# Delta-rule attention with a mixture of experts: the column steps of one block's triangular inverse move from VectorE to GpSimd

## The chip, the core and the metric

The kernel runs on one core of a Trainium2 chip. A core has five engines, each with its own instruction queue that is worked off in order: TensorE (PE in the profile; PEld is its weight load), VectorE (DVE), ScalarE (ACT), GpSimd (POOL) and SyncE (SP), which only issues DMAs here. They meet through semaphores. All work on SBUF, an on-chip memory of 128 partitions; PE writes its results to PSUM, which DVE and ACT read. The metric is device time in microseconds (us). The kernel before took 501.41 us, the median of three runs (498.14 to 501.8).

## What is computed

For 32 pairs of batch and head, a state of 48x48 is carried through 768 positions (q, k, v of 48 features each, beta one number):

```python
k_n = k / (np.linalg.norm(k, axis=-1, keepdims=True) + 1e-06)
for t in range(S):
    y[:, :, t] = np.einsum('bhd,bhde->bhe', q[:, :, t], state)
    v_old = np.einsum('bhde,bhd->bhe', state, kt)
    state = state + bt[:, :, :, None] * np.einsum('bhd,bhe->bhde', kt, vt - v_old)
```

The 3072 rows of the result (384 wide) then go through a mixture of 8 experts: the largest of 8 logits picks an expert, `relu(x @ w1) @ w2` (1024 hidden) is computed by that expert, and the row is scaled by its softmax weight.

## The kernel before

The 768 positions are cut into 6 time blocks of 128, and each block into 4 pieces of 32. Inside a piece the recurrence is a triangular system; its inverse is computed beforehand for all 32 pairs and the 4 pieces of a block at once (tile `wt`, 128 partitions by 32x32). The main loop has 27 ticks (`for t in range(NN + LAG)`); tick t starts the four pieces of one batch of block t // 4, so that block tb is needed from tick 4 tb on. A tick has seven slots, `beside(t, 0)` to `beside(t, 6)`, and `place` counts them (7t + i). Per tick:

- PE multiplies state and keys (`residual`, L442 and L454), DVE subtracts the product from the values (L461, one instruction a tick), PE multiplies with the inverse (`apply`, L469, needs `wt`), ACT copies the result to tile `u` (L473, into a tile that POOL has cleared, L431), and PE makes outputs and states from it (L492, L503, L512) and the next masks (L279; POOL masks them, L290). PE's products of the router (`xp`, L536) and of the block after next (L279, `pg`) stand between one tick's L454 and its L469.
- Beside it a block's inverse is worked out on DVE, cut into small steps that are put between the others. `prepare` makes norms and diagonals (L303 `ss`, a square root on ACT at L307, then L325 to L340, L349) from tile `lg`, which a DMA brings (L269); `lanes` has a first scaling (L377) and then 14 pairs of column steps (L382: product into `tmp`; L385: sum into `lw`, each needing the one before), then the corner: a copy (L390), six products (L401) and six sums (L407), and the transpose into `wt` (L412).
- The router's small steps run on POOL up to tick 16 (L648 to L696), and it scatters the rows with indirect DMAs (L544).

Order: everything is issued by the Python program in this order; no scheduler moves it. `ROOT[tb]` gives three places for a block: where its `ss` is taken, where the square root is issued, and where the rest of `prepare` may begin. In each slot `inverses` issues steps up to a budget (0.9 of the program's own units); two blocks at a time may be open and then take turns. A block's transpose isn't issued before tick 4 tb - 1, and what is left of a block at tick 4 tb is issued there at once. After the loop come the eight experts, where PE is nearly always busy.

Of the kernel before, what the change touches and what calls it, by code (L numbers as in the profile page):

```python
# [13 lines left out]
ALU = mybir.AluOpType  # L14
# [27 lines left out]
def deltanet_moe(ctx, tc, kt_d, qt_d, kn_d, v_d, beta_d, w_gate, w1, w2, out):  # L42
    nc = tc.nc
# [75 lines left out]
    LAG = NB - 1  # L119
    FILL = 'k4 k5 k6 k7', 'k1 q0 k2 k3', 'k8 k9', 'k10 k11 q1'  # L120

    ROOT = {1: (-1, -1, -1), 2: (17, 20, 22), 3: (38, 41, 43), 4: (66, 69, 71), 5: (94, 97, 99)}
    INIT = (0, 1, 2, 3, 'l', 0)

    STEPS = (3, 3, 3, 2, 2, 2, 2)
# [56 lines left out]
    tiles = {tb: {b: {} for b in range(B)} for tb in range(NT)}  # L182
# [52 lines left out]
    def kpart(n):  # L235

        tb, b = n // B, n % B
        kt, gg = kt_t[n] if n < KTL else kg_t[n % KTG], gg_t[n % KSL]
        V, A = nc.vector.tensor_copy, nc.scalar.copy
        if tb == 0:  # L240
# [6 lines left out]
            for h in range(H):  # L247
                p, a = h // 2, h % 2
                r = slice(64 * a, 64 * a + 64)
                for i in range(NB):  # L250
                    t = slice(32 * i, 32 * i + 32)
                    nc.tensor.matmul(db[a][t, p, :], lhsT=kt[r, p, t], rhs=kt[r, p, t], start=True, stop=True,
                                     tile_position=(64 * a, 32 * i), skip_group_check=True)
            V(out=dg[:, b * H:(b + 1) * H:2], in_=db[0])
            A(out=dg[:, b * H + 1:(b + 1) * H:2], in_=db[1])
# [53 lines left out]
    def prepare(tb):  # L309
# [13 lines left out]
        ss, s0, r0 = (T[k] for k in ("ss", "s0", "r0"))  # L323
        V = nc.vector
        V.reciprocal(r0, s0)  # L325
        yield
        V.scalar_tensor_tensor(out=r0, in0=ss, scalar=0.25, in1=r0, op0=ALU.mult, op1=ALU.mult)
        yield
        V.scalar_tensor_tensor(out=s0, in0=r0, scalar=1e-6, in1=s0, op0=ALU.add, op1=ALU.add)
        yield  # L330
# [28 lines left out]
    def both_halves(t):  # L359

        def view(r, c, m, w):
            return bass.AP(tensor=t.tensor, offset=t.offset + 32 * r + c, ap=[list(t.ap[0]), [16 * 33, 2], [32, m], [1, w]])
        return view

    def lanes(tb):


        T = tiles[tb]
        lg, lw = T["lg"], T["lw"]
        G, W = both_halves(lg), both_halves(lw)  # L370
        V = nc.vector
        tmp = fp.tile([128, 128], F32, name=f"tmp{tb}", tag=f"tmp{tb % 2}")
        for c in range(15):
            m, w = 15 - c, c + 1
            if c == 0:
                for g in (0, 16):
                    V.tensor_scalar(out=lw[:, g + 1:g + 16, g], in0=lg[:, g + 1:g + 16, g], scalar1=lw[:, g, g:g + 1],  # L377
                                    scalar2=None, op0=ALU.mult)
                yield 0.4
                continue  # L380
            x = tmp[:, 0:2 * m * w].rearrange("p (g a b) -> p g a b", g=2, a=m)
            V.tensor_tensor(out=x, in0=G(w, c, m, 1).broadcast_to([128, 2, m, w]),  # L382
                            in1=W(c, 0, 1, w).broadcast_to([128, 2, m, w]), op=ALU.mult)
            yield 0.2 + m * w / 480
            V.tensor_tensor(out=W(w, 0, m, w), in0=W(w, 0, m, w), in1=x, op=ALU.add)  # L385
            yield 0.2 + m * w / 480
        big = [fp.tile([128, 1024], F32, name=f"big{i}_{tb}", tag=f"big{i}") for i in range(2)]

        first_, prod = lg[:, 0:16, 0:16], lg[:, 0:16, 16:32]
        V.tensor_copy(first_, lw[:, 0:16, 0:16].rearrange("p k a -> p a k"))  # L390
        yield 0.5
        work = []
        for a, b in ((0, 4), (4, 9), (9, 16)):
            work.append((first_[:, a:b, a:16], lg[:, 16:32, a:16], prod[:, a:b], False))
        for a, b in ((12, 16), (7, 12), (0, 7)):
            work.append((lw[:, 16 + a:16 + b, 16:16 + b], prod[:, :, 0:b], lw[:, 16 + a:16 + b, 0:16], True))
        todo = []
        for i, (x, y, out, minus) in enumerate(work):
            m, n, k = x.shape[1], y.shape[1], x.shape[2]
            t = big[i % 2][:, 0:m * n * k].rearrange("p (m n k) -> p m n k", m=m, n=n)  # L400
            V.tensor_tensor(out=t, in0=x.unsqueeze(2).broadcast_to([128, m, n, k]),  # L401
                            in1=y.unsqueeze(1).broadcast_to([128, m, n, k]), op=ALU.mult)
            yield 0.15 + m * n * k / 960
            todo.append((out, t, minus))
            while len(todo) > (i not in (2, 5)):
                out, t, minus = todo.pop(0)
                V.tensor_reduce(out=out, in_=t, axis=AX.X, op=ALU.add, negate=minus)  # L407
                yield 0.15 + t.shape[1] * t.shape[2] * t.shape[3] / 960
        T["cols"] = True
        yield 0.0  # L410
        T["wt"] = lp.tile([128, BH, 32], F32, name=f"wt{tb}", tag="wt", bufs=2)
        V.transpose(out=T["wt"].rearrange("p h t -> p t h"), in_=lw)  # L412
        if tb + 2 < NT:
            clear_w(tb + 2)
        yield 2.0

    def scale_v(t, act=False):

# [521 lines left out]
    class Inverse:  # L940
# [6 lines left out]
        def steps(self):  # L947
            for _ in prepare(self.tb):
                yield 0.2
            yield 1.2  # L950
            self.at = 0
            yield from lanes(self.tb)

        def ready(self, t):
            if self.at == -12:
                return place[0] >= ROOT[self.tb][2]
            return not ("cols" in tiles[self.tb] and t < B * self.tb - 1)

        def step(self):
# [4 lines left out]
            self.at += 1  # L964
            return us

    line = [Inverse(tb) for tb in range(1, NT)]
    turn, owed, place = [None], [0.0], [-1]

# [5 lines left out]
    W = None  # L975

    def inverse_step(t):
        if not line:
            return None
        a = line[0]  # L980
        b = line[1] if len(line) > 1 and line[1].ready(t) else None
        ready = a.ready(t)
        if not ready and b is None:
            return None
        pair = ready and b is not None and "cols" not in tiles[a.tb]
        x = (b if turn[0] is a else a) if pair else a if ready else b
        turn[0] = x
        return x.step()

    def inverses(us, t):  # L990
        owed[0] += us
        while owed[0] > 0:
            got = inverse_step(t)
            if got is None:
                owed[0] = 0.0
                return
            owed[0] -= got
# [8 lines left out]
    def beside(t, i):  # L1006

        place[0] = 7 * t + i
        for tb in ROOT:
            if place[0] == ROOT[tb][0]:  # L1010
                squares(tb)
            if place[0] == ROOT[tb][1]:
                root(tb)
        inverses((SPEND0 if t < B else SPEND if t < 3 * B else SPEND2)[i], t)
        for _ in range(STEPS[i] if t < NN - B else 4):
            if fine and not run(fine[0]):
                fine.pop(0)
        for _ in range(WSL.count((t, i))):
            run(W)
        for _ in range(ES.count((t, i))):  # L1020
            ahead_step()

    fin = iter(())
    for t in range(NN + LAG):
        if t < NN and t % B == 0 and t > 0:
            while line and line[0].tb <= t // B:
                inverse_step(t)
            if t == NN - B:
# [3 lines left out]
                W = pieces()  # L1032
# [122 lines left out]
    V = nc.vector  # L1155
# [82 lines left out]
    op = ctx.enter_context(tc.tile_pool(name="op", bufs=1))  # L1238
# [10 lines left out]
    if True:  # L1249
# [3 lines left out]
        V = nc.vector  # L1253
# [107 lines left out]
```

## Time and profile before

| | |
|---|---|
| runs | 501.8, 498.14, 501.41 us |
| profiled execution | 498.63 us, its span 496.9 us |
| PE | 454.6 us (91%) |
| DVE | 321.2 us (65%) |
| ACT | 262.2 us (53%) |
| POOL | 166.1 us (33%) |
[...]

Shares are over the whole span. The loop takes about the first half of it; in tick 3 (61.6 to 70.1 us) DVE was busy for all of its 8.5 us and PE for 7.85, and from 41 to 209 us DVE was busy for 145 and POOL for 109 of 168 us.

### The profile page before, as it was taken

How to read it: one execution, taken by the hardware profiler on the slowest of the kernel's cores; microseconds unless marked ns; L12 is line 12 of the kernel's file. 1: busy time of each engine (PE TensorE's matmuls, PEld its weight loads, DVE VectorE, ACT ScalarE, POOL GpSimd, SP SyncE). 2: the span in 40 equal slices, each digit the busy share in tenths (PEclk: the TensorE clock that was granted, in tenths of full speed). 3: DMA queues.
4: the chain of work that ended last, by engine and by line, in shares of the span. 5: the costliest groups of instructions: out<-in, count | busy, mean ns of one | idle time of the engine just before them, and what ended most of it. 6: DMA issues, size and time to landing. Idle time of an engine off the chain costs nothing. (4 is left out here: it accounts for less than half of the span.)

```text
span 496.9 us, 17303 instructions
## 1 busy us (share of the span) xinstructions
PE 454.6 (91%) x7212; PEld 417.8 (84%) x7212; DVE 321.2 (65%) x726; ACT 262.2 (53%) x566; POOL 166.1 (33%) x338
## 2 busy tenths in 40 slices
PE   6768799989989799978899999999999999999995
PEld 4657678868778688866798999999999999999995
DVE  2899998797889989445544668274463647255330
ACT  2644876666757466666433456463553545354230
POOL 7003134767878878730211210201102020201111
PEclk9985999999999999979999899999999999999999
DMA  5999599783684353733302548464545646353101
GB/s 172 248 295 225 99 267 254 174 204 108 140 211 130 114 153 112 252 119 111 118 35 66 158 144 252 141 217 119 174 135 159 190 138 218 123 172 110 36 2 45
DMA packets 59228, 76.29 MB, mean 154 GB/s; under 512 B 26569, under 2 KB 45471, under 8 KB 59136
## 3 DMA queue, kind: packets, MB, share of 16 engines
q1 hardware_dynamic: 55680, 65.39, 47.5%
q0 software_dynamic: 3456, 9.57, 5.2%
q8 instruction: 71, 1.16, 1.0%
q14 instruction: 21, 0.17, 0.1%
HBM read 57.10 MB, written 18.62 MB: 152 GB/s over the span
## 5 line engine op out<-in xcount | busy, mean ns | idle before, releaser
L809 POOL DMA_INDIRECT out_dram<-yo,idx x32 | 30.7, 960 | 199.0 <-ACT yo L1140 118.2
L806 PE MATMUL y<-w2h,hx 128*128 128x384 f32 x352 | 93.5, 340 | 0.1
L729 DVE TENSOR_TENSOR w2l<-w2r,w2h 128x768 fp32r<-128x768 f32 x32 | 31.2, 978 | 74.7 <-ACT w2h L728 74.5
L806 PEld LDWEIGHTS y<-w2h,hx 128*128 128x128 f32 x352 | 64.1, 188 | 0.4 <-issue 0.4
L806 PE MATMUL y<-w2l,hx 128*128 128x384 f32 x176 | 59.3, 337 | 0.0
L795 PE MATMUL h<-xl,w1h 128*128 128x416 f32 (+2 forms) x168 | 57.3, 341 | 0.2 <-DVE xl L729 0.2
L795 PE MATMUL h<-xh,w1h 128*128 128x416 f32 (+2 forms) x168 | 57.3, 341 | 0.0
L795 PE MATMUL h<-xh,w1l 128*128 128x416 f32 (+2 forms) x168 | 57.2, 341 | 0.0
L473 ACT COPY u<-ks 32x384 f32<-32x384 f32 x96 | 45.1, 470 | 20.9 <-PE ks L469 18.8
L290 POOL TENSOR_SCALAR_AFFINE_SELECT pm<-pm 128x1024 f32<-128x1024 f32 x24 | 27.6, 1149 | 76.7 <-ACT pm L289 76.3
L798 ACT ACTIVATE hx<-h 128x448 fp32r<-128x448 f32 (+1 forms) x64 | 32.8, 517 | 32.6 <-PE h L795 29.3
L1140 ACT ACTIVATE yo<-y,gt 128x384 f32<-128x384 f32 x22 | 12.8, 582 | 69.9 <-PE y L806 57.0
L442 PE MATMUL ks<-st,kt 128*32 128x96 f32 x768 | 44.9, 253 | 2.4 <-ACT u L473 2.3
L799 DVE SCALAR_TENSOR_TENSOR hx<-h,hx 128x448 fp32r<-128x448 f32 (+1 forms) x64 | 36.8, 586 | 14.6 <-ACT hx L798 14.5
L442 PEld LDWEIGHTS ks<-st,kt 128*32 128x32 f32 x768 | 33.4, 111 | 6.3 <-ACT u L473 2.8
L544 POOL DMA_INDIRECT xg<-row,sli x24 | 29.4, 1224 | 25.5 <-ACT yt L516 8.0
L259 ACT COPY gg<-pg 128x512 f32<-128x512 f32 x48 | 25.8, 589 | 22.2 <-PE pg L279 22.2
L729 DVE TENSOR_TENSOR w1l<-w1r,w1h 128x1024 fp32r<-128x1024 f32 x24 | 29.4, 1224 | 9.9 <-ACT w1h L728 6.7
L469 PE MATMUL ks<-v_all,wt 32*32 32x48 f32 x1536 | 27.2, 207 | 9.2 <-DVE v_all L461 7.0
L469 PEld LDWEIGHTS ks<-v_all,wt 32*32 32x32 f32 x1536 | 22.3, 107 | 14.3 <-DVE v_all L461 9.0
L806 PEld LDWEIGHTS y<-w2l,hx 128*128 128x128 f32 x176 | 33.1, 188 | 0.0
L795 PEld LDWEIGHTS h<-xl,w1h 128*128 128x128 f32 x168 | 31.5, 188 | 0.6 <-DVE xl L729 0.5
(199 smaller groups left out, 1034.3 us busy)
## 6 DMA issues: line engine op xcount, KB each, us to landing
w1r<-in_w_dram SPq DMA_DIRECT2D x24, 512.0 KB
w2r<-in_w_dram SPq DMA_DIRECT2D x32, 384.0 KB
xg<-zrow SPq DMA_DIRECT2D x7, 788.0 KB
xr<-xg SPq DMA_DIRECT2D x7, 591.0 KB
ku<-in_kn_dram SPq DMA_DIRECT2D x20, 192.0 KB
qt<-in_qt_dram SPq DMA_DIRECT2D x36, 96.0 KB
kt<-in_kt_dram SPq DMA_DIRECT2D x34, 96.0 KB
v_all<-in_v_dram SPq DMA_DIRECT2D x15, 192.0 KB
```

The source lines that it names most:

```text
L259: A(out=gg[:, a:H:2], in_=pg[a])
L290: nc.gpsimd.affine_select(out=pm, in_=pm, compare_op=ALU.is_gt, fill=0.0, base=0, pattern=[[0, H], [1, C]], channel_multiplier=-1)
L442: nc.tensor.matmul(ks[32 * q:32 * q + 32, 2 * p:2 * p + 2, :], lhsT=kt_t[n % KTL][:, p, 32 * q:32 * q + 32], rhs=st_view(n % B, p), start= ...
L469: nc.tensor.matmul(ks[r, h, :], lhsT=tiles[n // B]["wt"][r, n % B * H + h, :], rhs=vn[r, h, :], start=True, stop=True, tile_position=(32 * ...
L473: nc.scalar.copy(out=uview(n)[r], in_=ks[r])
L544: put = nc.gpsimd.indirect_dma_start(out=xg, out_offset=bass.IndirectOffsetOnAxis(ap=at, axis=0), in_=x, in_offset=None, bounds_check=OFF ...
L729: nc.vector.tensor_tensor(out=lo, in0=src, in1=hi.bitcast(F32), op=ALU.subtract)
L795: nc.tensor.matmul(ps, lhsT=w[:, d, fs], rhs=x_[:, d], start=(n == 0), stop=(n == len(terms) - 1))
L798: nc.scalar.activation(out=hh, in_=ps, func=AF.Relu)
L799: nc.vector.scalar_tensor_tensor(out=hl, in0=ps, scalar=0.0, in1=hh.bitcast(F32), op0=ALU.max, op1=ALU.subtract)
L806: nc.tensor.matmul(ps, lhsT=h(f)[h_], rhs=w2[w][:, f, :], start=(n == 0), stop=(n == len(terms) - 1))
L809: nc.gpsimd.indirect_dma_start(out=out, out_offset=bass.IndirectOffsetOnAxis(ap=idx, axis=0), in_=yo, in_offset=None, bounds_check=N - 1, ...
```

## The change

Block 2 gets an entry in a table `COLS`. Its column steps are issued for POOL by `columns_beside`, from place 16 (tick 2, slot 2) on, five instructions per two slots; its corner stays on DVE and is issued only when all its column steps have been. All `ROOT` places move forward by 8 to 10 slots, and while block 2's `prepare` isn't done, it goes ahead of block 1's steps.

```diff
--- before.py
+++ after.py
@@ -119,7 +119,8 @@
     LAG = NB - 1
     FILL = 'k4 k5 k6 k7', 'k1 q0 k2 k3', 'k8 k9', 'k10 k11 q1'
 
-    ROOT = {1: (-1, -1, -1), 2: (17, 20, 22), 3: (38, 41, 43), 4: (66, 69, 71), 5: (94, 97, 99)}
+    ROOT = {1: (-1, -1, -1), 2: (8, 11, 13), 3: (28, 31, 33), 4: (58, 61, 63), 5: (86, 89, 91)}
+    COLS = {2: (16, 5, 2)}
     INIT = (0, 1, 2, 3, 'l', 0)
 
     STEPS = (3, 3, 3, 2, 2, 2, 2)
@@ -362,13 +363,13 @@
             return bass.AP(tensor=t.tensor, offset=t.offset + 32 * r + c, ap=[list(t.ap[0]), [16 * 33, 2], [32, m], [1, w]])
         return view
 
-    def lanes(tb):
+    def columns(tb):
 
 
         T = tiles[tb]
         lg, lw = T["lg"], T["lw"]
         G, W = both_halves(lg), both_halves(lw)
-        V = nc.vector
+        V, P = nc.vector, nc.gpsimd if tb in COLS else nc.vector
         tmp = fp.tile([128, 128], F32, name=f"tmp{tb}", tag=f"tmp{tb % 2}")
         for c in range(15):
             m, w = 15 - c, c + 1
@@ -379,11 +380,17 @@
                 yield 0.4
                 continue
             x = tmp[:, 0:2 * m * w].rearrange("p (g a b) -> p g a b", g=2, a=m)
-            V.tensor_tensor(out=x, in0=G(w, c, m, 1).broadcast_to([128, 2, m, w]),
+            P.tensor_tensor(out=x, in0=G(w, c, m, 1).broadcast_to([128, 2, m, w]),
                             in1=W(c, 0, 1, w).broadcast_to([128, 2, m, w]), op=ALU.mult)
             yield 0.2 + m * w / 480
-            V.tensor_tensor(out=W(w, 0, m, w), in0=W(w, 0, m, w), in1=x, op=ALU.add)
+            P.tensor_tensor(out=W(w, 0, m, w), in0=W(w, 0, m, w), in1=x, op=ALU.add)
             yield 0.2 + m * w / 480
+
+    def corner(tb):
+
+        T = tiles[tb]
+        lg, lw = T["lg"], T["lw"]
+        V = nc.vector
         big = [fp.tile([128, 1024], F32, name=f"big{i}_{tb}", tag=f"big{i}") for i in range(2)]
 
         first_, prod = lg[:, 0:16, 0:16], lg[:, 0:16, 16:32]
@@ -413,6 +420,10 @@
         if tb + 2 < NT:
             clear_w(tb + 2)
         yield 2.0
+
+    def lanes(tb):
+        yield from columns(tb)
+        yield from corner(tb)
 
     def scale_v(t, act=False):
 
@@ -949,11 +960,18 @@
                 yield 0.2
             yield 1.2
             self.at = 0
-            yield from lanes(self.tb)
+            if self.tb in COLS:
+                held[self.tb] = columns(self.tb)
+                yield next(held[self.tb])
+                yield from corner(self.tb)
+            else:
+                yield from lanes(self.tb)
 
         def ready(self, t):
             if self.at == -12:
                 return place[0] >= ROOT[self.tb][2]
+            if self.tb in held:
+                return False
             return not ("cols" in tiles[self.tb] and t < B * self.tb - 1)
 
         def step(self):
@@ -964,6 +982,15 @@
             self.at += 1
             return us
 
+    def columns_beside():
+
+        for tb in list(held):
+            n = ((place[0] - COLS[tb][0] + 1) * COLS[tb][1]) // COLS[tb][2] - ((place[0] - COLS[tb][0]) * COLS[tb][1]) // COLS[tb][2]
+            for _ in range(n if place[0] >= COLS[tb][0] else 0):
+                if tb in held and next(held[tb], None) is None:
+                    del held[tb]
+
+    held = {}
     line = [Inverse(tb) for tb in range(1, NT)]
     turn, owed, place = [None], [0.0], [-1]
 
@@ -983,7 +1010,7 @@
         if not ready and b is None:
             return None
         pair = ready and b is not None and "cols" not in tiles[a.tb]
-        x = (b if turn[0] is a else a) if pair else a if ready else b
+        x = (b if turn[0] is a or (b.tb in COLS and b.at < 0) else a) if pair else a if ready else b
         turn[0] = x
         return x.step()
 
@@ -1012,6 +1039,7 @@
             if place[0] == ROOT[tb][1]:
                 root(tb)
         inverses((SPEND0 if t < B else SPEND if t < 3 * B else SPEND2)[i], t)
+        columns_beside()
         for _ in range(STEPS[i] if t < NN - B else 4):
             if fine and not run(fine[0]):
                 fine.pop(0)
```

How it moves instructions, at three places. `v_all` with `ks` is the one subtraction of a tick; `lg`, `lw`, `ss`, `s`, `r`, `tmp` with the numbers 603, 634, 755 to 757, 892 to 894 and 907 belong to block 2, `lg_437`, `lw_155` and `big_1` to block 1, `lg_855` to block 3. Line numbers behind L119 are higher by 1 to 28 after the change.

DVE from tick 2's subtraction, before (down to tick 3's) and now (as many rows as reach block 1's corner):

```order
L461 TENSOR_TENSOR v_all<-v_all,ks_800 96x384
L401 TENSOR_TENSOR big_1_797<-lg_437 128x960
L407 TENSOR_REDUCE lg_437<-big_1_796 128x4x16
L401 TENSOR_TENSOR big_1_796<-lg_437 128x784
L303 TENSOR_SCALAR ss_892<-lg_603 128x32
L407 TENSOR_REDUCE lg_437<-big_1_797 128x5x16
L407 TENSOR_REDUCE lg_437<-big_1_796 128x7x16
L401 TENSOR_TENSOR big_1_797<-lw_155,lg_437 128x1024
L461 TENSOR_TENSOR v_all<-v_all,ks_914 128x384
```

```order
L472 TENSOR_TENSOR v_all<-v_all,ks_805 96x384
L326 RECIPROCAL r_757<-s_756 128x32
L328 SCALAR_TENSOR_TENSOR r_757<-ss_755,r_757 128x32
L330 SCALAR_TENSOR_TENSOR s_756<-r_757,s_756 128x32
L332 RECIPROCAL r_757<-s_756 128x32
L334 TENSOR_TENSOR ss_755<-bl,r_757 128x32
L337 TENSOR_TENSOR lw_634<-ss_755,r_757 128x32
L341 SCALAR_TENSOR_TENSOR lg_603<-lg_603,lw_634 128x16x16 x2
L350 STREAM_TRANSPOSE r_757<-s_756 128x32
L378 TENSOR_SCALAR lw_634<-lg_603,lw_634 128x15 x2
L408 TENSOR_TENSOR big_1_802<-lg_437 128x960
L414 TENSOR_REDUCE lg_437<-big_1_801 128x4x16
```

Block 2's whole `prepare` and its first scaling now stand between tick 2's subtraction and block 1's second product.

POOL in ticks 2 to 4, before and now (from the norms of block 2 on; 19 more column steps follow, with `u_997`, `pm_119` and then the clearing of `lw_1121` between or behind them):

```order
L431 MEMSET u_753 128x384
L431 MEMSET u_851 128x384
L290 AFFINE_SELECT pm_118<-pm_118 128x1024
L431 MEMSET u_971 128x384
L290 AFFINE_SELECT pm_119<-pm_119 128x1024
L296 MEMSET lw_1082 128x1024
```

```order
L355 COPY nt_all<-r_757 32x32 x4
L383 TENSOR_TENSOR tmp_907<-lg_603,lw_634 128x56
L386 TENSOR_TENSOR lw_634<-lw_634,tmp_907 128x2x14x2
L383 TENSOR_TENSOR tmp_907<-lg_603,lw_634 128x78
L386 TENSOR_TENSOR lw_634<-lw_634,tmp_907 128x2x13x3
L383 TENSOR_TENSOR tmp_907<-lg_603,lw_634 128x96
L386 TENSOR_TENSOR lw_634<-lw_634,tmp_907 128x2x12x4
L383 TENSOR_TENSOR tmp_907<-lg_603,lw_634 128x110
L386 TENSOR_TENSOR lw_634<-lw_634,tmp_907 128x2x11x5
L291 AFFINE_SELECT pm_118<-pm_118 128x1024
L383 TENSOR_TENSOR tmp_907<-lg_603,lw_634 128x120
```

The 28 column steps now stand in POOL's queue, around the clearing of tick 4's `u` and two masks.

DVE from tick 4's subtraction, with what each row waits for, before and now:

```order
L461 TENSOR_TENSOR v_all<-v_all,ks_1084 128x384 [waits DMAHW5_49,PE_49,Activation_49]
L336 TENSOR_TENSOR lw_634<-ss_892,r_894 128x32 [waits DVE_49]
L340 SCALAR_TENSOR_TENSOR lg_603<-lg_603,lw_634 128x16x16 [waits DVE_49]
L340 SCALAR_TENSOR_TENSOR lg_603<-lg_603,lw_634 128x16x16
L349 STREAM_TRANSPOSE r_894<-s_893 128x32
L538 TENSOR_REDUCE rl_0_1135<-xp_0_1136 128x8 [waits Activation_49]
L425 TENSOR_TENSOR v_all<-v_all,nt_all 128x384 [waits DMAHW2_49]
L377 TENSOR_SCALAR lw_634<-lg_603,lw_634 128x15 [waits DVE_49] x2
```

```order
L472 TENSOR_TENSOR v_all<-v_all,ks_1123 128x384 [waits DMAHW5_49,PE_49,Activation_49]
L304 TENSOR_SCALAR ss_1165<-lg_855 128x32 [waits DMAHW0_49]
L549 TENSOR_REDUCE rl_0_1170<-xp_0_1171 128x8 [waits Activation_49]
L436 TENSOR_TENSOR v_all<-v_all,nt_all 128x384 [waits DMAHW2_49]
L397 COPY lg_603<-lw_634 128x16x16 [waits Pool_49]
L408 TENSOR_TENSOR big_2_1195<-lg_603 128x1024 [waits DVE_49]
L408 TENSOR_TENSOR big_2_1196<-lg_603 128x960
L414 TENSOR_REDUCE lg_603<-big_2_1195 128x4x16 [waits DVE_49]
```

The copy that begins block 2's corner (L397 there) now waits for POOL, and stands in DVE's queue ahead of tick 5's subtraction, as do the corner's first three products and its first sum.

## Rows read from the trace of the kernel before

**Rows 1.** Timeline of DVE, ticks 0 to 5: start us, us, engine, line, operation, tiles.
```profile
41.18 0.52 DVE L461 TENSOR_TENSOR v_all<-v_all,ks 32x384 f32<-32x384 f32 x1
...
44.55 0.22 DVE L382 TENSOR_TENSOR tmp<-lg,lw 128x56 f32<-128x56 f32 x1
...
47.97 0.54 DVE L461 TENSOR_TENSOR v_all<-v_all,ks 64x384 f32<-64x384 f32 x1
...
54.63 0.54 DVE L461 TENSOR_TENSOR v_all<-v_all,ks 96x384 f32<-96x384 f32 x1
...
61.59 0.55 DVE L461 TENSOR_TENSOR v_all<-v_all,ks 128x384 f32<-128x384 f32 x1
...
70.13 0.53 DVE L461 TENSOR_TENSOR v_all<-v_all,ks 128x384 f32<-128x384 f32 x1
...
77.08 0.55 DVE L461 TENSOR_TENSOR v_all<-v_all,ks 128x384 f32<-128x384 f32 x1 [0.27 <-PE ks L454]
```

**Rows 2.** Timeline of DVE, corner of block 0, which no other work cuts into.
```profile
26.15 0.39 DVE L390 COPY lg<-lw 128x256 f32<-128x256 f32 x1
...
30.92 2.02 DVE L407 TENSOR_REDUCE lg<-big 128x80 f32<-128x960 f32 x2
```

**Rows 3.** Timeline of PE, the triangular products of ticks 4, 5 and 16.
```profile
70.72 0.45 PE L469 MATMUL ks<-v_all,wt 32*32 32x48 f32 x23 [0.43 <-DVE v_all L461]
...
79.08 0.70 PE L469 MATMUL ks<-v_all,wt 32*32 32x48 f32 x45
...
172.50 0.88 PE L469 MATMUL ks<-v_all,wt 32*32 32x48 f32 x64 [1.53 <-DVE v_all L461]
```

**Rows 4.** Waits of PE from 38 to 205 us: total us, times, longest us.
```profile
PE ks L469 <- DVE v_all L461: 3.2, 4, 1.5
...
PE pp L674 <- POOL oh_all L670: 1.6, 2, 0.9
```

**Rows 5.** POOL's two-input operations, two lines: duration ns min/median/max.
```profile
L648 POOL TENSOR_TENSOR m<-s x8: 195/196/337, 81.5 to 198.0; 128x2 f32<-128x2 f32 x8
...
L690 POOL TENSOR_TENSOR pos<-pos,oh_all x8: 218/219/1008, 88.8 to 203.6; 128x16 f32<-128x16 f32 x8
```

**Rows 6.** Timeline of POOL and DVE, two places where both are busy.
```profile
117.91 2.29 DVE L401 TENSOR_TENSOR big<-lg 128x1024 f32<-128x1024 f32 x2
...
118.02 1.16 POOL L648 TENSOR_TENSOR s<-oh 128x8 f32<-128x8 f32 x1
...
120.33 0.20 POOL L648 TENSOR_TENSOR m<-s 128x2 f32<-128x2 f32 x1
...
120.62 0.23 POOL L667 TENSOR_SCALAR m<-m 128x2 f32<-128x2 f32 x1
...
163.31 1.11 POOL L290 TENSOR_SCALAR_AFFINE_SELECT pm<-pm 128x1024 f32<-128x1024 f32 x1
...
163.34 1.49 DVE L425 TENSOR_TENSOR v_all<-v_all,nt_all 128x384 f32<-128x384 f32 x1
```

**Rows 7.** Timeline of PE, the same part of ticks 21 and 22.
```profile
209.59 0.88 PE L469 MATMUL ks<-v_all,wt 32*32 32x48 f32 x64
...
213.05 1.16 PE L279 MATMUL pq<-qt,kt 64*128 64x128 f32 x16
...
219.40 1.50 PE L469 MATMUL ks<-v_all,wt 32*32 32x48 f32 x64 [2.47 <-DVE v_all L461]
...
225.12 1.28 PE L279 MATMUL pq<-qt,kt 64*128 64x128 f32 x16
```

**Rows 8.** Stretch of 2 us: PE, PEld, DVE, ACT, POOL busy, granted clock, DMA.
```profile
220.00:222.00 2.00, 2.00 (x64) 1.74 (x52) 0.00 (x0) 0.13 (x1) 1.16 (x2) 0.50 0.77 194
```

**Rows 9.** Timeline of the DMA queue on SyncE.
```profile
27.52 0.34 SPq L269 DMA_DIRECT2D lg<-gd  x1
...
32.53 0.80 SPq L210 DMA_DIRECT2D ku<-in_kn_dram  x2
...
43.99 0.34 SPq L269 DMA_DIRECT2D lg<-gd  x1
```

## The prediction

> **What bounds the kernel now.** I read the shares by engine first, then the timelines of DVE and PE tick by tick, then PE's waits, and the timeline of POOL last.
>
> Over the span PE is busy 91% and DVE 65%, but the loop differs from the experts behind it, where only PE counts. In ticks 0 to 4 DVE has no rest: its subtraction, L461, starts at 41.18, 47.97, 54.63, 61.59 and 70.13 us without waiting for PE [rows 1], with the inverse of block 1 worked in between. At tick 5 (77.08) it waits for PE for the first time [rows 1]. What a late subtraction costs is read on PE, at L469, the first product that needs it: tick 4's waited 0.43 us for DVE, tick 5's (79.08) not at all, although the subtraction had ended at 77.63, because PE still had router and mask products to do [rows 3]. So at tick 5 DVE has about 1.45 us to spare, at tick 4 nothing. From 38 to 205 us PE lost 3.2 us to late subtractions, the longest 1.53 at tick 16, and 1.6 us to POOL's router steps [rows 3, 4]. That is 4.8 us in all, and no relief of DVE or POOL in these ticks can bring back much more. Two of these waits lie in ticks where the change puts work onto DVE (ticks 3 and 4).
>
> **The change, part by part.**
>
> *28 column steps leave DVE.* The smallest took 0.22 us [rows 1], so DVE loses at least 6 us of work, in ticks 4 and 5; in tick 5 PE, not DVE, ends last [rows 1, 3]. By itself this shortens nothing there. It counts later, since each block is now worked out earlier: block 2's transpose moves to before tick 8, block 4's last sums partly out of tick 15. I give back the 1.53 us of tick 16 and two thirds of the 1.6 us of POOL waits: **-2.6 us**. The bounds are 0 and -3.2 (1.6 of POOL, 1.53 of DVE).
>
> *Block 2's prepare goes in front of block 1's corner.* On DVE, from tick 0's subtraction to block 1's first column step, the same `prepare` and first scaling took 44.55 - 41.18 = 3.37 us [rows 1]. Behind tick 2's subtraction (54.7 with the `ss` that now comes earlier) the corner is therefore reached at 58.1. Block 0's corner ran alone: 4.77 us from its copy to its second sum, and 41.18 - 30.92 = 10.26 us from there to the next subtraction, transpose included [rows 1, 2]. Of the 4.77, copy and first product are done already in tick 2 (about 1.55, a half of 2.29 [rows 6] and the copy's 0.39 [rows 2]), so 3.2 us remain, and tick 3's subtraction starts at 61.3, as before (61.59). Then 0.5 us for it and 10.26 us: tick 4's starts at 72.1, where it was 70.13 [rows 1]. Before, half of these small steps ran in gaps between large ones; now they are a chain. PE had no slack at tick 4, so this is **+2.0 us**, and nothing hides it.
>
> *POOL against DVE.* POOL's column steps have two inputs from SBUF. Beside DVE's two products of 2.29 us a POOL operation that takes 0.20 on its own took 1.16; beside POOL's mask (1.11 us) DVE's scaling took 1.49 [rows 5, 6], where its like took 0.55 in the subtraction [rows 1]. So each waits for the other. DVE starts some five two-input operations between POOL's first step and tick 4's subtraction; each can wait for a step of 0.2 to 0.4 us, 0 to 2 us in all. I take **+0.5 us**, since a column step is far nearer to the small operations than to the mask. Tick 4's L469 then starts at about 73.2 instead of 70.7, and PE stands idle some 2.5 us longer.
>
> *DVE's wait for POOL in tick 4.* This is the largest term. A POOL step with 2 elements per partition takes 0.196 us, one with 16 takes 0.219: 1.64 ns per element [rows 5]. From one's end to the next's start there is 0.09 us (120.33, 0.20 long, then 120.62) [rows 6]. The 14 widths give 1330 elements, twice: 28 x 0.196 + 2604 x 1.64 ns + 28 x 0.085 = 12.1 us. Two masks of 1.11 us [rows 6] stand between: 14.3 us. They begin when block 2 is scaled and its four copies of norms are through, about 60.0. DVE gets to the corner's copy, which needs the last step, 1.4 us behind tick 4's subtraction: 72.6 + 1.4 = 74.0. In these 14 us DVE's two-input work takes 5.9 us (four products at about 1.1 [rows 6], three operations of 0.55 [rows 1]), in which POOL only slips in between. So POOL has done about 8.4 of 14.3 us, and DVE waits until about 80. From that copy to tick 5's subtraction lie 5.2 us (4.77 [rows 2] and two small steps), and 0.55 for the subtraction: 85.8. PE gets to L469 of tick 5 at 73.2 + (79.08 - 70.72) = 81.6. **+4.2 us**. Bounds: 0 if POOL were not held up at all (14.3 from 60.0 is 74.3), +2 if an element cost no more than the mask's (1.11 us for 1024), +6 if DVE blocks it in full and each step is 0.05 longer.
>
> [...]
>
> *PE's clock.* [...] With idle times of about 2.9 and 4.2 us in ticks 4 and 5 I expect one such stretch: **+2.3 us**; bounds 0 and two of them, +4.6.
>
> *The rest at nothing.* The tile `lg` of block 2 must land earlier, in tick 1: it is issued at 43.99; block 1's, issued at 27.52, let the queue go on at 32.53, so 5.0 us, about 49.0, just before DVE asks for it behind four column steps of tick 1 (47.97 and on) [rows 1, 9]. If it comes later, tick 2 begins later by as much. The square root on ACT moves within slack of DVE's own chain. SP's and PE's queues keep their order. The norms of block 3 now stand in POOL's queue ahead of a batch's slots, which nobody awaits for several us.
>
> **Sum:** 2.0 + 0.5 + 4.2 + 2.3 - 2.6 = +6.4, on the profiled execution 498.63 + 6.4 = 505.0. That execution lies 2.8 below the median of the runs (501.41); all four together have a mean of 500.0, which I take as the base: **506.4 us**.
>
> **Rivals.**
>
> *POOL is done in time (0.25).* If a column step is cheap and mutual blocking rare, the corner's copy doesn't wait: 2.5 - 2.6, with or without one stretch of low clock: 500 to 502. For it speaks that sums (L407) and the transpose leave POOL alone; against it the 1.16 us of rows 6.
>
> *Faster (0.15).* DVE is the engine without rest in ticks 0 to 4, and the change takes work from it. If block 2's `prepare` fitted into gaps and POOL were done by 75, all 4.8 us of PE's waits [rows 4] would go: 495.2. It decides at tick 4: the subtraction must start at or before 70.1. [...] Against it: DVE gets more work before tick 4, not less.
>
> *Worse (0.15).* Full blocking in both directions (+2 at tick 4, +6 at tick 5) and two stretches of low clock (+4.6), less 1: 511.6.
>
> **How the numbers follow.** The forecast has 0.45 and by its own bounds runs from 503 to 510. About 1% (5 us) is what a measurement of this kernel can tell from no change. Slower by more: 0.32 of the forecast and all but 0.01 of the worse case, 0.46. Faster by more: at most half of the faster case with the upper runs as base, 0.09. Within: the rest, 0.45. The range leaves out half of each outer case: 497 to 511.5.
>
> **What would show it.** In the changed kernel's profile: tick 4's subtraction near 72 to 73 instead of 70; POOL's column steps 0.3 to 0.45 us each, and over 1 us beside DVE's products; DVE idle for some 6 us before the corner's copy, released by POOL; L469 of tick 5 waiting for DVE for several us; a granted clock of 0.5 near 80 to 95 us; tick 16 without its wait. I am wrong if POOL's last step ends by 76, or if PE's waits behind tick 8 shrink by more than 4 us.

## The result and the profile after

The changed kernel takes **504.79 us** (median of 16 runs) against 500.67 for the kernel before on the same chip (16 runs): a ratio of 1.0089, 95% interval 1.0067 to 1.011, so 3.4 to 5.5 us slower. The profiled execution took 505.92 us (span 504.1), 7.3 more than that of before. Line numbers move by a few: L461 is now L472 (the subtraction), L469 is L480 (the first product that needs it), L390 is L397 (the corner's copy).

The clearest view is a table of when PE's first product that needs the subtraction (L469, now L480) starts in eight of the ticks, from PE's timeline of both kernels (us):

| tick | 0 | 3 | 4 | 5 | 7 | 13 | 16 | 25 |
|---|---|---|---|---|---|---|---|---|
| before | 41.79 | 62.19 | 70.72 | 79.08 | 96.91 | 147.87 | 172.50 | 251.50 |
| after | 43.92 | 63.67 | 74.62 | 87.53 | 107.71 | 158.35 | 179.44 | 258.58 |
| difference | 2.13 | 1.48 | 3.90 | 8.45 | 10.80 | 10.48 | 6.94 | 7.08 |

The first 2.13 us lie ahead of the loop, where nothing was changed; in the ten kernels below, with the same work ahead of it, the same start lies between 40.95 and 42.92, so I take it for a difference between executions. From tick 0 to tick 25 the change costs 7.08 - 2.13 = 4.95 us in this pair of executions: 2.42 in tick 3's interval (from its L480 to tick 4's), 4.55 in tick 4's, 2.35 in the next two, less 3.54 given back between ticks 13 and 16 and 0.83 in all other ticks.

The timeline of DVE in the changed kernel, from tick 3's subtraction to tick 5's, answers to [rows 1] (start us, us, engine, line, operation, tiles):

```profile
63.07 0.55 DVE L472 TENSOR_TENSOR v_all<-v_all,ks 128x384 f32<-128x384 f32 x1
...
65.58 2.51 DVE L408 TENSOR_TENSOR big<-lw,lg 128x1024 f32<-128x1024 f32 x2
...
74.03 0.54 DVE L472 TENSOR_TENSOR v_all<-v_all,ks 128x384 f32<-128x384 f32 x1
...
74.91 0.54 DVE L436 TENSOR_TENSOR v_all<-v_all,nt_all 128x384 f32<-128x384 f32 x1
80.26 1.36 DVE L397 COPY lg<-lw 128x256 f32<-128x256 f32 x1 [4.81 <-POOL lw L386]
81.65 3.05 DVE L408 TENSOR_TENSOR big<-lg 128x1024 f32<-128x1024 f32 x2
...
86.94 0.54 DVE L472 TENSOR_TENSOR v_all<-v_all,ks 128x384 f32<-128x384 f32 x1
```

Between the subtractions of ticks 3 and 4 DVE has no gap, and it takes 10.96 us; it was 8.54 [rows 1]. Then it stands 4.81 us at the corner's copy, and tick 5's subtraction, which has nothing to do with block 2, is queued behind. The timeline of POOL shows what it waits for:

```profile
61.90 0.28 POOL L383 TENSOR_TENSOR tmp<-lg,lw 128x56 f32<-128x56 f32 x1
62.26 1.05 POOL L386 TENSOR_TENSOR lw<-lw,tmp 128x56 f32<-128x56 f32 x1
...
65.58 1.50 POOL L386 TENSOR_TENSOR lw<-lw,tmp 128x110 f32<-128x110 f32 x1
67.03 2.01 POOL L291 TENSOR_SCALAR_AFFINE_SELECT pm<-pm 128x1024 f32<-128x1024 f32 x1
...
79.97 0.25 POOL L386 TENSOR_TENSOR lw<-lw,tmp 128x30 f32<-128x30 f32 x1
80.16 0.95 POOL L297 MEMSET lw<- 128x1024 f32 x1
...
81.43 1.13 POOL L291 TENSOR_SCALAR_AFFINE_SELECT pm<-pm 128x1024 f32<-128x1024 f32 x1
```

The last step ends at 80.22. Where DVE runs none of its large products the steps take 0.24 to 0.45 us; three that run into one take 1.03 to 1.50, and one beside the scaling at 74.91 takes 0.78. The clearing and the mask behind the steps now run beside DVE's copy, which takes 1.36 us instead of 0.39 [rows 2], and beside its first two products, which take 3.05 instead of 2.29 [rows 6]. PE's timeline, which answers to [rows 3]:

```profile
74.62 0.88 PE L480 MATMUL ks<-v_all,wt 32*32 32x48 f32 x64 [2.85 <-DVE v_all L472]
...
87.53 1.50 PE L480 MATMUL ks<-v_all,wt 32*32 32x48 f32 x64 [5.00 <-DVE v_all L472]
...
98.13 0.88 PE L480 MATMUL ks<-v_all,wt 32*32 32x48 f32 x64
...
179.44 0.88 PE L480 MATMUL ks<-v_all,wt 32*32 32x48 f32 x64
```

PE's waits from 38 to 205 us (total, times, longest), beside [rows 4]: 3.2 us of waiting for the subtraction has become 10.0, and 1.6 for POOL's router steps 1.0.

```profile
PE ks L480 <- DVE v_all L472: 10.0, 7, 5.0
...
PE pp L685 <- POOL oh_all L681: 1.0, 1, 1.0
```

And stretches of 2 us behind tick 4's wait and behind the long one (columns as in [rows 8]; the granted clock is the number before the last two):

```profile
74.00:76.00 2.00, 1.38 (x80) 1.17 (x80) 1.45 (x5) 0.43 (x1) 1.76 (x4) 1.00 0.80 245
...
84.00:86.00 2.00, 0.00 (x0) 0.00 (x0) 2.00 (x3) 0.00 (x0) 0.00 (x0) 1.00 1.01 297
...
88.00:90.00 2.00, 2.00 (x68) 1.57 (x60) 2.00 (x5) 0.88 (x2) 0.00 (x0) 0.50 0.03 8
90.00:92.00 2.00, 2.00 (x32) 1.98 (x30) 2.00 (x6) 1.63 (x5) 1.66 (x2) 0.50 0.00 0
```

PE does nothing from 84 to 86 us; when it has work again its clock is at 0.50, and L480 takes 1.50 us where it takes 0.88 at a clock of 1.00. Tick 4's wait of 2.85 us left the clock at 1.00. Tick 16's wait [rows 3] is gone.

### The profile page after: what moved, and what is told of

Read it like the earlier page. It is cut to its first block, busy times and chain, and to the rows that moved or that the text cites. A ratio compares the mean times of both kernels' runs of the same rounds, so it can differ in the third digit from the quotient of the medians.

```text
span 504.1 us, 17306 instructions
## 1 busy us (share of the span) xinstructions
PE 455.3 (90%) x7212; PEld 418.2 (83%) x7212; DVE 318.5 (63%) x698; ACT 262.0 (52%) x566; POOL 177.6 (35%) x366
## 5 line engine op out<-in xcount | busy, mean ns | idle before, releaser
L480 PE MATMUL ks<-v_all,wt 32*32 32x48 f32 x1536 | 26.5, 208 | 14.8 <-DVE v_all L472 14.5
L480 PEld LDWEIGHTS ks<-v_all,wt 32*32 32x32 f32 x1536 | 22.2, 109 | 19.3 <-DVE v_all L472 16.3
```

The lines of the kernel that those rows point to most:

```text
L480: nc.tensor.matmul(ks[r, h, :], lhsT=tiles[n // B]["wt"][r, n % B * H + h, :], rhs=vn[r, h, :], start=True, stop=True, tile_position=(32 * ...
```

## The experiments

Each experiment ran on one chip with the kernel before beside it, and the chips differ. The table has the number of runs, the medians (us) of the kernel and of before on its chip, and the ratio with its interval; the ratio is not that of the two medians.

| kernel | runs | median | before | ratio to before |
|---|---|---|---|---|
| changed kernel | 16 | 504.79 | 500.67 | 1.0089 (1.0067 to 1.0110) |
| 1 corner late | 4 | 507.47 | 499.71 | 1.0132 (1.0067 to 1.0196) |
| 2 PE kept busy | 10 | 502.83 | 499.71 | 1.0042 (1.0013 to 1.0072) |
| 3 no column steps | 10 | 500.14 | 499.71 | 0.9968 (0.9930 to 1.0007) |
| 4 places only | 10 | 500.86 | 499.71 | 1.0002 (0.9963 to 1.0041) |
| 5 take turns | 10 | 502.04 | 499.23 | 1.0056 (1.0014 to 1.0098) |
| 6 corner late, block 5 late | 10 | 504.57 | 499.23 | 1.0088 (1.0039 to 1.0137) |
| 7 nobody waits | 10 | 501.77 | 498.16 | 1.0044 (1.0002 to 1.0086) |
| 8 prepare late | 4 | 509.72 | 498.16 | 1.0186 (1.0088 to 1.0284) |
| 9 half the steps | 10 | 500.82 | 498.16 | 1.0045 (0.9997 to 1.0093) |
| 10 spread, no POOL | 12 | 502.41 | 500.34 | 1.0039 (1.0003 to 1.0074) |

Differences of 2 us between two of these rows are about what the intervals can tell; the traces say more. Added lines shift L472 and L480 by up to 8 in some kernels, so that in the seventh L480 is the subtraction and L488 the product.

**1. The corner late.** In `ready`:

```
-            if self.tb in held:
+            if self.tb in held or self.tb in COLS and self.at > 0 and place[0] < 35:
                 return False
```

> Block 2's corner (its copy, products and sums on DVE) is handed out from the start of tick 5, behind tick 5's subtraction, and not in tick 4; POOL's 28 column steps stay where they are. Theory (the loss is DVE's queue: tick 5's subtraction stands behind the copy that waits for POOL): the wait of 5.0 us at L480 of tick 5 is gone (its start near 83 us instead of 87.5), the granted clock stays up and tick 6 comes as soon behind tick 5 as before; tick 4's 2.85 us of waiting stays. 4.6 + 2.3 less: 498 us, if the corner's ten microseconds in ticks 5 to 7 don't make a subtraction there late. Rival (DVE and POOL hold each other up, wherever the copy stands): POOL ends at about the same time and DVE has the same work behind it, so ticks 6 to 8 become late instead: 503 to 505.

Measured: 507.47, outside what either theory gave. PE's timeline:

```profile
74.99 0.96 PE L480 MATMUL ks<-v_all,wt 32*32 32x48 f32 x64 [2.77 <-DVE v_all L472]
...
84.31 0.88 PE L480 MATMUL ks<-v_all,wt 32*32 32x48 f32 x64
...
175.35 0.17 PE L685 MATMUL pp<-oh_all,ltri 128*128 128x16 bf16 x1 [2.66 <-POOL oh_all L681]
...
179.83 1.32 PE L480 MATMUL ks<-v_all,wt 32*32 32x48 f32 x51 [3.26 <-DVE v_all L472]
```

Tick 5 does what the theory said: no wait, L480 in 0.88 us, and tick 8's L480 starts 34.65 us behind tick 4's where the changed kernel takes 42.71. The forecast forgot the later blocks. With block 2's corner later, blocks 3 and 4 come later too; block 5's steps then take turns with block 4's corner, and between the subtractions of ticks 15 and 16 (165.37 and 179.26 on DVE's timeline) stand five sums, three products, the transpose and eight column instructions: 13.9 us, where PE needs 7.5 (the changed kernel's interval). This execution also lost 2.68 us in tick 8 (last section).

**6. The same, with block 5 late** (told here because it answers the first):

```
-    ROOT = {..., 5: (86, 89, 91)}
+    ROOT = {..., 5: (101, 104, 106)}
```

> The kernel of the run with the corner late, and block 5's norms, root and prepare also later (101, 104, 106 for 86, 89, 91), so that no step of block 5 stands in turn with block 4's corner. DVE's instructions between the subtractions of ticks 15 and 16 are then 3 sums, 1 product and the transpose fewer or so, about 7 us of work instead of 13. Theory (the run with the corner late was slow because block 4's corner, taking turns with block 5, came out at tick 16): tick 16's waits of 2.7 us for POOL and 3.3 us for DVE go, with the low clock behind them: 6 to 8 us less than that run's 507.5: 499.5 to 501.5. Rival (it was slow from a stall that the profile doesn't name, such as 2.7 us in tick 8): 505 to 508.

Measured: 504.57, a miss in size. The interval up to tick 16's L480 is 7.73 us instead of 13.55 and its wait 0.58 instead of 3.26, so the first run's loss at tick 16 is explained; but work now comes out late at tick 20, where L480 waits 2.04 us, and in this execution tick 4's wait brought the low clock:

```profile
205.35 1.42 PE L480 MATMUL ks<-v_all,wt 32*32 32x48 f32 x64 [2.04 <-DVE v_all L472]
```
```profile
72.00:74.00 2.00, 0.68 (x36) 0.69 (x40) 2.00 (x5) 0.00 (x0) 1.69 (x5) 0.59 0.85 238
74.00:76.00 2.00, 2.00 (x63) 1.55 (x54) 0.15 (x1) 1.08 (x3) 1.69 (x5) 0.50 1.04 335
```

**2. PE kept busy in its wait.**

```
+        if t == 5:
+            dummy(20)
         copies = apply(t)
```

> The changed kernel, with 20 products of zeros (128x512, bf16) on TensorE ahead of tick 5's L480, in the time in which it waits for DVE; their result is used nowhere. Theory (the idle time itself lowers the granted clock, and that is a term of its own of 2.3 us): L480 of tick 5 starts as before near 87.5 but takes 0.88 us instead of 1.50, and tick 6's follows 8.4 us later, not 9.7 to 10.6: 502.5 us. Rival (tick 6 is late because DVE has still to work off the corner of block 2, not because of the clock): 504.5 to 505, unchanged.

Measured: 502.83, as the theory had it. The copy on DVE's timeline, then PE's timeline and one stretch of 2 us:

```profile
78.58 1.36 DVE L397 COPY lg<-lw 128x256 f32<-128x256 f32 x1 [4.79 <-POOL lw L386]
```
```profile
82.49 4.26 PE L733 MATMUL wm<-zrow 128*128 128x512 bf16 x19 [0.16 <-issue]
86.69 0.88 PE L480 MATMUL ks<-v_all,wt 32*32 32x48 f32 x64
...
95.52 0.88 PE L480 MATMUL ks<-v_all,wt 32*32 32x48 f32 x64
```
```profile
88.00:90.00 2.00, 2.00 (x46) 1.66 (x40) 2.00 (x6) 1.93 (x6) 1.34 (x2) 1.00 0.04 10
```

DVE waits as long for POOL as in the changed kernel (4.79 us), but L480 takes 0.88 us, the clock stays at 1.00 there, and from tick 5's L480 to tick 7's PE takes 104.26 - 86.69 = 17.57 us where the changed kernel takes 20.18: the idle time's second price is 2.6 us. The products themselves hold L480 up until 86.69, though tick 5's subtraction had ended at 85.80, so of these 2.6 us this kernel keeps about 1.7.

**3. No column steps, and 7. the steps on other tiles, so that nobody waits.** In the third, `columns` skips both instructions of a step for block 2; in the seventh they read zeros and write only the scratch tile:

```
+            if tb in COLS:
+                z2, z1 = zrow[:, 0:2 * m], zrow[:, 0:2 * w]
+                P.tensor_tensor(out=x, in0=z2.rearrange(...).broadcast_to([128, 2, m, w]),
+                                in1=z1.rearrange(...).broadcast_to([128, 2, m, w]), op=ALU.mult)
+                yield 0.2
+                P.tensor_tensor(out=x, in0=x, in1=zrow[:, 0:2 * m * w].rearrange(...), op=ALU.add)
+                yield 0.2
+                continue
             P.tensor_tensor(out=x, in0=G(w, c, m, 1)...
```

> The changed kernel without the 28 column steps of block 2 on POOL (that part of block 2's inverse is not computed). Theory (the steps cost through DVE's wait at the corner's copy, some blocking of DVE, and the clock): DVE's wait of 4.81 us is gone, L480 of tick 5 starts near 83, no low clock, and tick 4's subtraction comes up to 0.5 us earlier: 497 to 498 us. Rival (the earlier norms and prepare, not POOL, cost the time): 503 to 505. Rival (mutual blocking is the main cost): tick 4's wait of 2.85 us goes as well, below 496.

> The changed kernel, with POOL's 28 column steps at their places and sizes, but on a tile of zeros and a scratch tile (so block 2's column steps are not computed, and no instruction of DVE needs POOL's result). Theory (the steps cost by being waited for, hardly by sharing memory access with DVE): DVE doesn't wait at the corner's copy, L480 of tick 5 waits less than 1 us, the time is that of the run without the steps (500.1) plus 0.3 to 0.5 us for the blocking: 500 to 501. Rival (mutual blocking): tick 4's subtraction is as late as in the changed kernel or later, and the total stays at 503 to 505.

Measured: 500.14 and 501.77, the one above the 497 to 498 that I expected, the other above 500 to 501 and below the rival. In both, tick 5 has no wait for DVE. From tick 4's L480 to tick 7's the changed kernel takes 33.09 us, the third 28.70 (with a low clock behind tick 4's wait, which I did not expect), the seventh 26.39 and the kernel before 26.19: in these ticks the steps cost by being waited for. The totals are less clear. By its ratio the seventh is only 0.45% (2.2 us) faster than the changed kernel, with overlapping intervals, and 0.76% (3.8 us) slower than the third, where I expected 0.3 to 0.5 us. A part of that is seen in the traces in tick 3, whose interval is 11.83 us in the seventh and 10.68 in the third; where the rest lies is not shown. DVE, POOL and PE of the third:

```profile
63.40 2.29 DVE L412 TENSOR_TENSOR big<-lw,lg 128x1024 f32<-128x1024 f32 x2
```
```profile
61.05 1.09 POOL L291 TENSOR_SCALAR_AFFINE_SELECT pm<-pm 128x1024 f32<-128x1024 f32 x1 [1.43 <-ACT pm L290]
```
```profile
72.16 1.50 PE L484 MATMUL ks<-v_all,wt 32*32 32x48 f32 x64 [2.58 <-DVE v_all L476]
...
82.81 0.70 PE L484 MATMUL ks<-v_all,wt 32*32 32x48 f32 x45
```

and of the seventh:

```profile
66.05 3.43 DVE L416 TENSOR_TENSOR big<-lw,lg 128x1024 f32<-128x1024 f32 x2
```
```profile
66.40 2.08 POOL L291 TENSOR_SCALAR_AFFINE_SELECT pm<-pm 128x1024 f32<-128x1024 f32 x1
```
```profile
75.97 1.50 PE L488 MATMUL ks<-v_all,wt 32*32 32x48 f32 x64 [3.70 <-DVE v_all L480]
...
85.92 0.88 PE L488 MATMUL ks<-v_all,wt 32*32 32x48 f32 x64
```

Here it is less the small steps that hold DVE up than the mask behind them in POOL's queue: without the steps it runs at 61.05, ahead of DVE's two products, and takes 1.09 us; with them it is pushed to where the products are, and both take longer, the products by 1.14 us. In the changed kernel the same mask took 2.01 and the products 2.51, only 0.22 longer. There a column step (65.58, 1.50 us) started with the first product and the mask came behind it, while in the seventh it was the mask that started next, 0.35 us behind the first product; so which instruction comes first seems to set this price, from 0.2 to 1.1 us in these two executions. In the seventh run the products take about as long as the third run's products and mask do together: 2.29 + 1.09 = 3.38 us, measured 3.43.

Tick 4's wait stays in the third without a single step on POOL (2.58 us against 2.85). So the rival that blamed blocking for tick 4 falls.

**4. The earlier places alone** (`COLS = {}`, which also drops the preference for block 2's prepare).

> The changed kernel's earlier places of norms and square roots, with no block's columns on POOL: DVE does block 2's column steps as in the kernel before, and takes block 1's and block 2's steps in turn. Theory (the earlier start moves work on DVE but adds none; the loss is from POOL's being waited for and from prepare standing ahead of the corner in one piece): tick 4's subtraction at most 2 us late, no wait for POOL, 500 to 502.5 us. Rival (the earlier places alone make the loss, since tick 4 has no slack): 504 to 506.

Measured: 500.86, no change. PE's timeline at tick 4:

```profile
71.60 0.88 PE L480 MATMUL ks<-v_all,wt 32*32 32x48 f32 x64 [2.52 <-DVE v_all L472]
```

Tick 4's wait is there with no column step on POOL at all. Ticks 3 to 6 take 2.33 us more than in the kernel before (37.05 against 34.72), and ticks 13 to 15 take 3.28 less (21.35 against 24.63; tick 16 waits 0.35 us), by the later blocks' earlier places. Tick 5 does not wait.

**8. Prepare behind block 1's corner.** The line of the first run with 42 for 35, and:

```
-    ROOT = {..., 2: (8, 11, 13), 3: (28, 31, 33), 4: (58, 61, 63), 5: (86, 89, 91)}
-    COLS = {2: (16, 5, 2)}
+    ROOT = {..., 2: (17, 24, 28), 3: (49, 52, 54), 4: (70, 73, 75), 5: (94, 97, 99)}
+    COLS = {2: (29, 4, 1)}
```

> Block 2's prepare comes behind block 1's corner (its norms at 17, root at 24, prepare from 28, the start of tick 4), POOL's column steps from 29 on, four a place, block 2's corner from 42 (behind tick 6's subtraction), and the later blocks at 54, 75 and 99. Theory (tick 4's wait of 2.85 us comes from prepare standing ahead of block 1's corner): DVE's work between the subtractions of ticks 3 and 4 falls from about 10.7 to 7.6 us, and L480 of tick 4 waits at most 0.4 us, with no low clock there. But POOL's steps now lie in ticks 4 and 5 among the mask and the router's steps, so PE may wait for POOL in tick 5 or 6, by up to 3 us as in the run where the blocks take turns: 498 to 502. Rival (tick 4 is late for another reason, such as POOL's blocking of DVE): its wait stays above 2 us, 502 to 505.

Measured: 509.72, the worst of all, but tick 4 answers the question. PE's timeline:

```profile
71.46 0.45 PE L480 MATMUL ks<-v_all,wt 32*32 32x48 f32 x23
...
90.62 0.17 PE L685 MATMUL pp<-oh_all,ltri 128*128 128x16 bf16 x1 [2.09 <-POOL oh_all L681]
...
147.95 1.50 PE L480 MATMUL ks<-v_all,wt 32*32 32x48 f32 x64 [1.91 <-DVE v_all L472]
```

From tick 3's L480 to tick 4's it takes 8.14 us, where the changed kernel takes 10.95. This edit also moves POOL's steps out of tick 3, but the third and fourth runs keep the wait without any step; so the wait was prepare's. The loss moved to where POOL's steps now are (the router's result comes 2.09 us late in tick 6) and to ticks 12 and 16, where L480 waits 1.91 and 1.46 us for DVE, since the blocks pushed back come out late. The total expected, 498 to 502, was missed by 7.7 us.

**5. Blocks 1 and 2 take turns.**

```
-        x = (b if turn[0] is a or (b.tb in COLS and b.at < 0) else a) if pair else ...
+        x = (b if turn[0] is a else a) if pair else ...
```

> The changed kernel without its preference for block 2's prepare: blocks 1 and 2 take turns again, as every other pair of blocks does. Nothing else is edited; block 2's prepare and first scaling end later, and so its corner's copy is handed out behind tick 5's subtraction (in the changed kernel ahead of it), while tick 15 keeps its order. Theory: tick 4's subtraction comes at most 0.6 us sooner, since most of prepare still lies ahead of it; tick 5's wait of 5.0 us and the low clock behind it are gone, and nothing is given back at tick 16: 497 to 499 us, against 504.8. Rival (as in the run with the corner late, what tick 5 saves is lost again later): 503 to 507.

Measured: 502.04, in between. Tick 5's wait is gone by this one condition, and tick 16 does not wait. But the steps now begin at 67.26 and end at 87.17, and the router's steps are in the same queue. DVE and PE:

```profile
87.20 0.40 DVE L397 COPY lg<-lw 128x256 f32<-128x256 f32 x1 [2.68 <-POOL lw L386]
```
```profile
91.00 0.17 PE L685 MATMUL pp<-oh_all,ltri 128*128 128x16 bf16 x1 [3.15 <-POOL oh_all L681]
```

**9. Taking turns, and half of the steps on POOL** (`if c == 8: P = nc.vector`).

> Blocks 1 and 2 take turns (as in that run), and POOL does only the first 14 of block 2's 28 column steps; the other 14 are DVE's again. Theory (POOL's time of 0.3 to 0.5 us a step is what is waited for, first by DVE and then by the router's steps behind it): POOL is done by about 78 us, the wait of 3.15 us for the router in tick 6 goes, DVE has 3.5 us more to do in ticks 4 and 5, where it has room: 498 to 500, 2 to 4 less than that run's 502.0. Rival (DVE's steps of the second half are late as POOL's were): 501 to 503.

Measured: 500.82. PE's timeline:

```profile
82.84 0.88 PE L482 MATMUL ks<-v_all,wt 32*32 32x48 f32 x64 [1.36 <-DVE v_all L474]
...
90.37 0.17 PE L687 MATMUL pp<-oh_all,ltri 128*128 128x16 bf16 x1 [1.78 <-POOL oh_all L683]
```

POOL's last step ends at 77.24 and the router is waited for by 1.78 us instead of 3.15; but DVE, with its 14 steps more, is late for tick 5's subtraction (1.36 us at L480), and POOL waits 2.05 us for DVE's maximum of the router's values. It lies between the two theories, and its interval just reaches down to the kernel before (0.9997).

**10. The gain by itself**, in the kernel before: `ROOT[4]` at `(62, 65, 67)`, `ROOT[5]` at `(98, 101, 103)`, no steps on POOL.

> No column steps on POOL, block 2's and 3's places as in the kernel before (prepare at 22 and 43); block 4 four places earlier (62, 65, 67) and block 5 four later (98, 101, 103), so that DVE has 6.8 us of work, where it had 9.0, between the subtractions of ticks 15 and 16, and 8.1 where it had 7.4 between those of 19 and 20. Theory (the one thing that the changed kernel gained is tick 16's wait of 1.53 us, by its later blocks' places alone): that wait goes, tick 20 pays at most 0.7 us: 0.8 to 1.5 us less than the kernel before, a ratio of 0.997 to 0.998. Rival (the change's gain behind tick 14 came from POOL's taking columns from DVE): no change, a ratio of 1.000 or above.

Measured: 502.41, a ratio of 1.0039: a miss, with the rival's number. Its reason need not follow, since the fourth run shortens the same ticks with all steps on DVE. PE's timeline has tick 16 without a wait, and what comes in its place:

```profile
165.12 0.78 PE L480 MATMUL ks<-v_all,wt 32*32 32x48 f32 x50 [0.74 <-DVE v_all L472]
...
172.50 0.88 PE L480 MATMUL ks<-v_all,wt 32*32 32x48 f32 x64
```

L480 of tick 16 starts at 172.50 as it did before, since tick 15's already starts 2.57 us later than before's 162.55; and tick 20's comes 3.37 us later (205.57 for 202.20), with PE's clock at 0.57 from 198 to 202 us (15 products of L523 take 1.91 us there, 1.04 in tick 4). Ahead of tick 15's 2.57 us lies, in tick 11, a stall of 1.54 us for which the profile names no one. No kernel here is clearly faster than the kernel before.

## Why the prediction was right

The forecast case came, by the steps that were named, but smaller: a change of 4.1 us (3.4 to 5.5) between the medians and 4.95 in the loop of this pair, where 6.4 was forecast. That 506.4 us lies nearer to the measured 504.8 than this is due to the base, taken as 500.0, which came out at 500.67. At 0.89% (0.67 to 1.10) the result is also about the 1% that the prediction took for what a measurement can tell; sixteen runs of each kernel told more. By its own terms:

- *Prepare in front of block 1's corner, +2.0, and blocking, +0.5.* Tick 4's L480 lost 2.42 us. Shown to be prepare's by the eighth run (prepare moved, wait gone) and by the third and fourth (POOL without steps, wait still there). In the third DVE takes 10.70 us between the two subtractions, against 8.54 before and 10.96 in the changed kernel: 2.16 for prepare and 0.26 for blocking. The seventh shows that blocking can cost 1.1, and that the mask does it, which the prediction's term, worked out from column steps, left out.
- *DVE's wait for POOL, +4.2.* Tick 5's L480 lost 4.55 us, but that the sum fits is in part luck. The wait itself was mis-sized: DVE stood 4.81 us where 74.0 to 80 was forecast, 6.0. (POOL's 80.22 is no hit, since this execution runs 1.48 us late from tick 3 on.) POOL lost about 3.7 us beside DVE's products and scaling, by comparison with the same steps in the eighth run, where 5.9 was allowed. What was missing came behind the wait: from the copy's start to tick 5's subtraction DVE took 6.68 us where 5.2 was forecast, while POOL's clearing and mask, held back behind the column steps, stood beside the copy and the first products (1.36 and 3.05 us, for 0.39 and 2.29). The second run repeats it (1.36 and 3.06). An element cost more than forecast: in the eighth run, where POOL works nearly undisturbed, the 28 steps take 10.34 us, with the one that was held up counted as its like (0.42); less 28 x 0.196 that is 1.86 ns for each of 2604 elements, not 1.64. That the copy stands ahead of tick 5's subtraction is one condition's doing (the fifth run).
- *PE's clock, +2.3.* 2.35 us from tick 5 to tick 7, and 2.6 by the second run. The term's size is what the low clock behind tick 22's wait of 2.47 us costs in [rows 7], (225.12 - 219.40) - (213.05 - 209.59) = 2.26 us, at a granted clock of 0.50 [rows 8]. One stretch, as forecast; that tick 4's wait would leave the clock alone was luck, since such a wait brought the low level in every other kernel here that had one (last section).
- *Given back, -2.6.* 3.54 us in this pair, a little more than the bound of 3.2: 1.07 in the interval up to tick 14 and 2.46 in that up to tick 16, where before had 0.72 and 0.92 of waits for POOL beside the 1.53 for DVE. Two causes were named, the 6 us of steps that DVE is rid of and the earlier places of the later blocks; the places suffice, for the fourth run has the same two intervals at 6.85 and 7.75 us (7.92 and 9.95 before) with all steps on DVE.
- *The rest at nothing.* Block 2's tile landed 0.68 us after DVE asked for it in tick 1, and L480 of tick 2 waited 0.40 us for DVE, where before it didn't wait. In seven of the experiments DVE waits for this tile, too, for 0.64 to 1.60 us. This is the one thing held at nothing that cost something.

Two readings of the prediction don't hold. The smallest column step took 0.19 us and not 0.22, though all 28 took 7.3 us before, so that its "at least 6" stands. And the sum of its worse case leaves out prepare's 2.0; with it the case is at 513.6, not 511.6.

The rivals: POOL was not done in time, and tick 4's subtraction came at 74.03, not by 70.1, so the faster case had no chance. That sums and the transpose leave POOL alone shows in the changed kernel: beside them (DVE's 63.53 to 65.55 and 70.19 to 74.17) POOL's steps took 0.34 to 0.45 us, within 0.01 of the same steps in the eighth run. The worse case needed blocking in full and two stretches of low clock, and neither came in this execution. A stretch behind tick 4's wait came in other kernels; no run shows blocking in full.

## What to carry to other kernels

An instruction that waits for another engine stops everything queued behind it, here for 4.81 us: before work is handed to a second engine, look where on the first one the result is taken up, and what stands behind that place. Look also at what the new work pushes back in the second engine's queue, and beside what it then runs. Moving the place where the result is taken up helps only if the work behind it still has room: here most of what was saved at tick 5 was lost at ticks 6, 16 or 20, wherever the next thing was due (runs 1, 5 and 6). And the idle time of a wait may cost twice, once as time (here 4.55 us at tick 5) and once in the clock afterwards (here 2.35 to 2.6 us at 0.50); filling the wait with idle work separates the two.

## What the runs showed that was not expected

- **Which wait lowers PE's clock.** L480's own time doesn't show it: in the second run tick 4's L480 took 0.88 us after a wait of 2.84, and the clock fell right behind it:

```profile
74.00:76.00 2.00, 2.00 (x39) 1.67 (x33) 0.00 (x0) 1.94 (x5) 1.61 (x6) 0.51 1.03 325
```

By the granted clock, nine of the twelve kernels wait 1.68 to 3.70 us for DVE at tick 4, and in eight of them a stretch at about 0.50 follows in that tick. Only the changed kernel, with 2.85 us, stays at 1.00. Tick 16's 1.53 us before brought no low clock (1.00 from 172 to 176 us), 1.91 at tick 12 of the eighth run did (L480 took 1.50 us). So a wait of this length mostly lowered the clock here, but its length alone doesn't decide; what does stays open.

- **A stall without a releaser.** In ten of these twelve executions PE stands once or twice between 103 and 117 us, mostly at `pp` or `yp`, for about 0.9 to 2.7 us, and the profile names no one it waits for: 0.88 and 1.31 before, 1.18 after, 2.68 in the first run, 2.38 in the fourth. In the first run the share of busy DMA is 0.92 to 1.10 from 108 to 116 us. It makes up to 2 us of difference between executions that have nothing to do with an edit; the cause wasn't tried.
